# A planned attention and feed-forward kernel: DMA lags in its planner, and the first pair of heads prepared in another way

## The chip, the cores and the metric

The kernel runs on one core of a Trainium2 chip. The metric is the device time of one execution in microseconds (us).

## The reference

Attention over 4 batches with 8 heads of 64 columns and 1152 rows, with the queries averaged over pairs of rows (576 are left), then a feed-forward layer with softplus, 512 to 2048 to 512, over the 2304 rows that result:

```python
q_pool = q.reshape(B, H, S // factor, factor, D).mean(axis=3)
scores = scale * np.matmul(q_pool, k.transpose(0, 1, 3, 2))
scores = scores - np.max(scores, axis=-1, keepdims=True)
attn = np.exp(scores)
attn = attn / (np.sum(attn, axis=-1, keepdims=True) + 1e-09)
return np.matmul(attn, v).astype(np.float32)
...
h = x @ w_in
g = np.maximum(h, 0.0) + np.log1p(np.exp(-np.abs(h)))
return (g @ w_out).astype(np.float32)
```

Inputs are float64 for the weights (decoded on the chip from 64-bit words) and the weights' products are made in float16 parts, high and low, so that the result keeps float32 accuracy.

## The kernel before

**Pairs and blocks.** The work is 16 pairs of heads (u0 to u15, four to a batch) and 8 blocks of tokens. `prepare` (L629) loads keys, queries and V of a pair, finds scales from sums of squares (`scale_from_squares` L369: a matmul with ones, four small VectorE steps), and splits keys and queries into float16 parts: a high part (`hi_ways` L398, on ScalarE, GpSimd or VectorE) and a remainder (`lo_ways` L416). The parts are transposed: for pair 0 by TensorE with copies out of PSUM (`turned` L707), for the others by a DMA on the sync queue (`kT`, `qA`). The second half of the keys is copied to `kB` by two more DMAs. `kD` is the difference of two groups of four key tiles.

**Maxima and shift.** `maxima` (L797) finds an upper bound of each score row ahead of attention, nine row tiles to a pair in two halves. `row` (L808) multiplies a query tile with `kD` and with the first keys; ScalarE takes Relu of the one, and a combined VectorE pass (L822) adds the other and takes the row's maximum. `last_keys` does the ninth key tile. The negated maximum is written as two extra columns of `qlow`, which is transposed into `qB`, so that a second score matmul with `kB` takes the shift away and adds the query remainder.

**Attention.** `attention` (L928) takes a pair in two halves (256 and 320 query columns) of nine key tiles: scores on TensorE, Exp on ScalarE (L958), the product with V on TensorE (L967). Sums of the exponentials are made in one of two ways. For the pairs in `SUMMED` TensorE multiplies them with ones (L983), two steps at a time; for the others GpSimd or VectorE adds them up (`tt_ways` L431, line L435), and one matmul per half (L1038) totals the result. The sums go through three small DMAs (`few`, `scratch`, `rinv`) and come back as reciprocals. `feed_forward` splits a block, multiplies it with w_in (s<-xh,w1h and two more), takes Softplus (L1199), splits again and multiplies with w_out.

**What sets the order.** Nothing is issued by hand. Every step is a task with one or several engines it may run on, a cost for each, buffers it takes and gives, tasks it depends on and a priority. `Sched.run` (L132) plays the tasks on a model of the engines: whenever an engine is free it takes the ready task of lowest priority value, unless another engine is expected to end it sooner, and the instruction is emitted then. Its numbers are `LAG` (from the end of a task on one engine to the start of a dependent one on another), `HEAD` (how much earlier a task that uses the port shared by VectorE and GpSimd may begin before the other engine's use of it ends), `LANDS` and the cost functions. `NUDGE` shifts the priority of each kind of task of each pair or block, and `LEAN` adds to an engine's cost where a task has a choice. All engines, the sync queue among them, then run their instructions in that order and wait on semaphores. `ORDER` sets where blocks stand: u0 to u4, then block 0's first matmuls (U0), u5 and u6 with its second ones (D0), U1, and so on.

## Time and profile before

| | |
|---|---|
| Median of 3 runs | 853.09 us (852.1 to 857.29) |
| Profiled execution | 852.98 us, of which the span from first to last instruction is 851.3 us |
| Mean granted clock of TensorE | 0.989 |

In a table by stretch, the first column is the stretch in us from the span's start, then its length; then for each engine the busy time in it and the number of instructions: PE is TensorE (matmul), PEld its weight loads, DVE VectorE, ACT ScalarE, POOL GpSimd. The last three columns are the granted clock as a share of full speed, the mean busy share of the DMA engines and GB/s. A group of instructions has its line and engine, what it writes and reads, its count, and after the bar its busy time in us and the mean of one in ns. A timeline row has its start and its length in us. A line number can be that of a helper: most matmuls are issued in L363, and small VectorE steps in L352 and L355.

### The profile page before, as it was taken

Reading aid. Unit: us, or ns where it says so; the run is one execution under the profiler, and the core shown is the slowest. Engines: PE = TensorE matmul, PEld = TensorE weight load, DVE = VectorE, ACT = ScalarE, POOL = GpSimd, SP = SyncE. Lnnn points to the kernel's source line nnn. Section 1 sums busy time; section 2 is a strip of 40 time slices with the busy share of each in tenths; the row PEclk is TensorE's granted clock in tenths of the full one; section 3 lists DMA queues with packets and bytes.
Section 4 is the critical chain, followed back from the end, with each engine's and each line's share of the span. In section 5 each row is a group of like instructions: output and inputs, shape, how many; then the busy total and the mean of one; then the engine's idle time right before and its main releaser. Section 6 shows DMA issues by size and latency. Waiting matters only on the chain.

```text
span 851.3 us, 24268 instructions
## 1 busy us (share of the span) xinstructions
PE 804.3 (94%) x10250; PEld 579.0 (68%) x10250; DVE 539.0 (63%) x1171; ACT 492.8 (58%) x823; POOL 317.5 (37%) x272
## 2 busy tenths in 40 slices
PE   3898898989899999999999999999999999999997
PEld 2465566558767688768666787667876678775754
DVE  7778888889998876675685643466556626012520
ACT  4788899889897427562665545457865572120210
POOL 0105418521249201331676514611268882090000
PEclk9899999999999999999999999999999999999999
DMA  8718657358664710411652330420603000000000
GB/s 306 163 36 215 146 169 203 114 127 186 173 134 139 120 54 2 125 28 46 125 78 79 90 79 13 83 89 19 94 13 92 22 15 10 22 15 25 2 14 25
DMA packets 98093, 74.23 MB, mean 87 GB/s; under 512 B 64960, under 2 KB 79296, under 8 KB 97984
## 3 DMA queue, kind: packets, MB, share of 16 engines
q1 hardware_dynamic: 97984, 72.68, 34.6%
q8 instruction: 80, 1.31, 0.7%
q14 instruction: 29, 0.24, 0.1%
HBM read 49.81 MB, written 4.79 MB: 64 GB/s over the span
## 4 chain that ended last, share of the span: by engine, by line
PE 69%; DVE 11%; ACT 6%; DMA 5%; POOL 5%; issue 3%; SPq 1%; ACTq 0%; DVEq 0%; POOLq 0%
PE s L363 30%; PE m L363 26%; PE pv L967 12%; POOL acc L435 3%; DMA kT<-kcat 2%; ACT p L958 2%; PE pv L983 2%; DMA raw<-in_k_dram 1%; ACT raw L523 1%; DVE w L355 1%; DVE qlow L355 1%; DVE kcat L355 1%; DVE g L822 1%; PE m L1038 1%; DVE acc L435 1%
## 5 line engine op out<-in xcount | busy, mean ns | idle before, releaser
L958 ACT ACTIVATE p<-s,cols 128x512 f32<-128x512 f32 (+1 forms) x288 | 208.3, 741 | 79.1 <-PE s L363 44.0
L435 POOL TENSOR_TENSOR acc<-acc,p 128x512 f32<-128x512 f32 (+1 forms) x122 | 183.9, 1507 | 119.3 <-ACT p L958 78.1
L967 PE MATMUL pv<-p,v 128*64 128x320 f32 (+1 forms) x1152 | 189.6, 416 | 1.3 <-ACT rinv L1046 0.8
L363 PE MATMUL m<-w,gh 128*64 128x512 f16 x1152 | 175.9, 379 | 0.1
L363 PE MATMUL s<-qA,kT 128*64 128x320 f16 (+1 forms) x1152 | 159.0, 289 | 6.0 <-ACT p L958 5.5
L363 PE MATMUL s<-qB,kB 66*64 66x320 f16 (+1 forms) x1152 | 159.5, 289 | 0.0
L822 DVE CUSTOM_DVE_ANT_0 g<-m,g 128x512 f32<-128x512 f32 x144 | 98.1, 686 | 67.4 <-ACT g L818 37.4
L1199 ACT ACTIVATE g<-s,blk 128x512 f32<-128x512 f32 (+1 forms) x80 | 51.3, 642 | 148.5 <-PE s L363 113.4
L363 PEld LDWEIGHTS <-w1h 128*64 128x64 f16 x2048 | 117.6, 110 | 14.8 <-issue 1.6
L363 PE MATMUL m<-w,gl 128*64 128x512 f16 x576 | 113.5, 379 | 0.0
L363 PEld LDWEIGHTS <-gh 128*64 128x64 f16 x1152 | 71.3, 110 | 46.7 <-issue 0.7
L363 PEld LDWEIGHTS <-kT 128*64 128x64 f16 x1152 | 80.1, 111 | 31.9 <-issue 12.9
L818 ACT ACTIVATE g<-m 128x512 f32<-128x512 f32 x144 | 84.8, 596 | 26.7 <-PE m L363 22.5
L967 PEld LDWEIGHTS pv<-p,v 128*64 128x64 f32 x1152 | 77.7, 138 | 30.5 <-issue 11.2
L363 PEld LDWEIGHTS <-kB 66*64 66x64 f16 x1152 | 75.2, 111 | 19.9 <-issue 5.4
L363 PE MATMUL s<-xh,w1h 128*64 128x256 f16 (+1 forms) x1024 | 85.6, 286 | 0.3 <-ACT g L1199 0.2
L363 PE MATMUL s<-xh,w1l 128*64 128x256 f16 (+1 forms) x1024 | 85.5, 286 | 0.0
L363 PE MATMUL s<-xl,w1h 128*64 128x256 f16 (+1 forms) x1024 | 85.5, 286 | 0.0
L363 PEld LDWEIGHTS <-qA 128*64 128x64 f16 x864 | 52.6, 112 | 38.3 <-issue 20.7
L363 PE MATMUL m<-kT,qA 128*64 128x128 f16 (+1 forms) x576 | 74.7, 310 | 3.9 <-ACT g L818 2.0
L363 PE MATMUL m<-kD,qA 128*64 128x512 f16 x288 | 60.0, 397 | 5.6 <-DVE nm L822 3.4
L363 PEld LDWEIGHTS <-w1l 128*64 128x64 f16 x1024 | 59.8, 110 | 4.3
(147 smaller groups left out, 960.8 us busy)
## 6 DMA issues: line engine op xcount, KB each, us to landing
raw<-in_k_dram SPq DMA_DIRECT2D x16, 576.0 KB
v<-in_v_dram SPq DMA_DIRECT2D x16, 576.0 KB
raw<-in_q_dram SPq DMA_DIRECT2D x64, 128.0 KB
raw<-in_moe_w_out_dram SPq DMA_DIRECT2D x16, 512.0 KB
kB<-kT SPq DMA_DIRECT2D x32, 144.0 KB
gh<-in_moe_w_in_dram SPq DMA_DIRECT2D x4, 1024.0 KB
gl<-in_moe_w_in_dram SPq DMA_DIRECT2D x4, 1024.0 KB
out_dram<-g SPq DMA_DIRECT2D x16, 256.0 KB
```

What stands on the lines that cost most here:

```text
L355: nc.vector.scalar_tensor_tensor(out=out_, in0=in0, scalar=s, in1=in1, op0=op0, op1=op1)
L363: nc.tensor.matmul(out=out_[c:e], lhsT=lhsT[:, c:e], rhs=rhs, start=start, stop=stop, tile_position=(0, at + c))
L435: e.tensor_tensor(out=o, in0=a, in1=b, op=op)
L523: nc.scalar.activation(out=o, in_=i, func=ACTF.Square, accum_out=am)
L818: r = task([("ACT", act(512, 1), lambda: nc.scalar.activation(out=rest.item, in_=more.item, func=ACTF.Relu))], [y], prio, take=[rest], giv ...
L822: parts.append(task([("DVE", dve(512, 1.0, 1), lambda: nc.vector.tensor_tensor_reduce(out=rest.item, in0=most.item, in1=rest.item, scale=1 ...
L958: nc.scalar.activation(out=pt.item[:, :, 0:n], in_=s.item[:, :, 0:n], func=ACTF.Exp, scale=x.sc)
L967: nc.tensor.matmul(out=pv.item[h * 64:(h + 1) * 64, 0:n], lhsT=x.v.item[:, h, kt], rhs=pt.item[:, h, 0:n], start=(kt == 0), stop=(kt == KT ...
L983: nc.tensor.matmul(out=pv.item[g:g + 32, 512 - n // 2:512], lhsT=ones[:, 0:32], rhs=pt.item[:, h, a * n // 2:(a + 1) * n // 2], start=Fals ...
L1038: nc.tensor.matmul(out=ps.item[g:g + 32, 512 - n // 2:512], lhsT=ones[:, 0:32], rhs=acc.item[:, h, a * n // 2:(a + 1) * n // 2], start=Tru ...
L1199: x = task([("ACT", act(N, 1, 1), lambda: nc.scalar.activation(out=gs.item[:, 0:N], in_=ps.item[:, 0, 0:N], func=ACTF.Softplus, scale=ih[: ...
```

## The change

- **Lags in the planner.** The lag from an engine to a DMA falls from 1250 to 1400 ns to 60 to 150 ns, that from a DMA to an engine from 100 to 50 ns; each DMA's issue is counted 95 ns longer. `HEAD` falls from 195 (VectorE) and 330 (GpSimd) to 140; more small tasks are marked as users of the shared port. `NUDGE` and `LEAN` are replaced as a whole.
- **The first pair.** Keys and queries of pair 0 get their scales by two chains of steps instead of one.
- **Loads held.** V of later pairs, the w_in loads and the loads of pair 2 wait until the high keys of pair 0 are copied to `kB`; loads of later pairs wait until the raw buffers of the pair before are used up. The throw-away output of V's squares goes to a buffer of the exponentials (`p`) instead of a raw one.
- **Two row tiles with plain maxima.** For tiles 1 and 5 of pair 0 `whole_row` multiplies the query tile with all eight key tiles into a score buffer, and VectorE takes the maximum of 1024 columns.
- **Four summed pairs.** 0, 1, 2, 3 instead of 0, 2, 4.
- **Order of attention.** Each score task depends on the one before it and each Exp on the one before it. The scale of a block's Softplus is waited for by its first matmul instead of by the Softplus.
- **The two extra columns** of `qlow` stand ahead of the remainder instead of behind it, so a transpose reads two overlapping strips and two memsets on GpSimd go.

```diff
     LAG = {
-        "PE": {"DVE": 200.0, "ACT": 200.0, "PE": 0.0, "DMA": 1300.0},
-        "DVE": {"DVE": 40.0, "ACT": 45.0, "POOL": 60.0, "PE": 55.0, "DMA": 1400.0},
-        "ACT": {"DVE": 45.0, "ACT": 40.0, "POOL": 60.0, "PE": 55.0, "DMA": 1250.0},
-        "POOL": {"DVE": 50.0, "ACT": 60.0, "POOL": 50.0, "PE": 60.0, "DMA": 1300.0},
-        "DMA": {"DVE": 100.0, "ACT": 100.0, "POOL": 100.0, "PE": 100.0, "DMA": 150.0},
+        "PE": {"DVE": 200.0, "ACT": 200.0, "PE": 0.0, "DMA": 150.0},
+        "DVE": {"DVE": 40.0, "ACT": 45.0, "POOL": 60.0, "PE": 55.0, "DMA": 60.0},
+        "ACT": {"DVE": 45.0, "ACT": 40.0, "POOL": 60.0, "PE": 55.0, "DMA": 80.0},
+        "POOL": {"DVE": 50.0, "ACT": 60.0, "POOL": 50.0, "PE": 60.0, "DMA": 130.0},
+        "DMA": {"DVE": 50.0, "ACT": 50.0, "POOL": 50.0, "PE": 50.0, "DMA": 40.0},
     }
...
-    HEAD = {"DVE": 195.0, "POOL": 330.0}
+    HEAD = {"DVE": 140.0, "POOL": 140.0}
...
 NUDGE = {
-    "prep": [-1.5, 0, 3.75, 1, -3.25, 18.5, -0.75, 0, 0, -23.5, 26, 6.75, 0.25, 3, 6.75, 8.75],
+    "prep": [0.5, 4.25, -6.5, 0.75, 1, -15, -3, 0, 17.25, 13.25, 32.5, 0, 14.25, 35.5, 5.75, 4],
...
-    SUMMED = (0, 2, 4)
+    SUMMED = (0, 1, 2, 3)
+    PLAIN = {0:(1,5)}
...
-            390.0, 2000. * W64, last_on[g % 2], prio, [])
+            390.0, 2000. * W64, last_on[g % 2] + [units[0].kB_done], prio, [])
...
-            400.0, 2340., [], prio - 6.0, [r])
+            400.0, 2340., units[u - 1].raw_free if u > 2 else [units[0].kB_done] if u == 2 else [], prio - 6.0, [r])
...
-        both = scale_from_squares(
-            cols[:, u, 0:2], cols[:, u, 2:4], cols[:, u, 4:6], cols[:, u, 6:8], [y, z], prio)
...
+        if u == 0:
+            both = scale_from_squares(c[0], c[2], c[4], c[6], [z], prio)
+            q_scale = scale_from_squares(c[1], c[3], c[5], c[7], [y], prio)
...
-        y = task(hi_ways(1152, lambda: (qc.item, twice(qs()), c[5]), ("ACT", "DVE")), [both], prio)
+        y = task(hi_ways(1152, lambda: (qc.item, twice(qs()), c[5]), ("ACT", "DVE")), [q_scale], prio)
...
-            400.0, 2340., [], prio, [x.v])
-        jk = Hold(raw_r)
+            400.0, 2340., [units[0].kB_done] if u else [], prio, [x.v])
+        jk = Hold(p_r)
...
         def row(c, t, heads, prio):
+            if c in x.plain:
+                return whole_row(c, heads, prio)
...
+        def whole_row(c, heads, prio):
+            ps = Hold(s_r)
...
+            y = scored_by(pe(2, 512), [c], mm, [d for h in heads for e in (0, 1) for d in k_of(x, h, e)], prio, [ps], [x.qA, x.kT])
+            parts.append(task([("DVE", dve(1024), lambda: nc.vector.tensor_reduce(
+                out=x.nm3.item[:, c, 0:1], in_=ps.item.rearrange("p a b -> p (a b)"), axis=AX.X, op=ALU.max))],
+                [y], prio, give=[ps]))
...
-                e = task([("ACT", act(2 * n, 1, 1), exp, "exp")], [y, x.sc_done, *gate], prio, take=[pt], give=[s])
+                scored_last[:] = [y]
+                e = task([("ACT", act(2 * n, 1, 1), exp, "exp")], [y, x.sc_done, *gate, *in_turn], prio, take=[pt], give=[s])
                 exps.setdefault(x.u, []).append(e)
+                in_turn[:] = [e]
```

What the planner made of it, counted in the two built programs:

| Instructions | before | after |
|---|---|---|
| matmuls of exponentials with ones (TensorE) | 216 | 288 |
| additions of exponentials on GpSimd | 136 | 75 |
| additions of exponentials on VectorE | 72 | 117 |
| key differences `kD` on GpSimd / VectorE | 12 / 20 | 2 / 30 |
| all instructions on GpSimd | 277 | 194 |
| all instructions on VectorE | 1173 | 1222 |
| all instructions on ScalarE | 753 | 769 |

(A matmul in float32 stands twice in the trace, so the 216 are 432 there.)

The first place is VectorE in pair 0, from the first scale to the keys' last copy. Names: `cols` holds the scales, `raw1_73` the queries, `raw0_72` the keys, `kcat` and `qcat` the float16 parts, `kT` and `qA` the transposed keys and queries. Before:

```order
L380 RECIPROCAL cols_120<-cols_120 128x2
L352 TENSOR_SCALAR cols_120<-cols_120 128x1
L352 TENSOR_SCALAR kcat0_78<-raw0_72,cols_120 128x9x64
L352 TENSOR_SCALAR qcat0_84<-raw1_73,cols_120 128x1152
L355 SCALAR_TENSOR_TENSOR kcat0_78<-raw0_72,cols_120,kcat0_78 128x9x64 x2
L355 SCALAR_TENSOR_TENSOR qlow0_85<-raw1_73,cols_120,qcat0_84 128x9x64
L728 CAST kT0_79<-m0_108 128x512
```

After, on the same engine, from the key remainders to the scaled queries:

```order
L351 SCALAR_TENSOR_TENSOR kcat0_78<-raw0_72,cols_120,kcat0_78 128x9x64 x2
L734 CAST kT0_79<-m1_109 128x512
L348 TENSOR_SCALAR cols_120<-m2_110 128x1
L734 CAST kT0_79<-m0_108 128x512
L348 TENSOR_SCALAR cols_120<-cols_120 128x1
L432 TENSOR_TENSOR kD0_81<-kT0_79 128x512
L348 TENSOR_SCALAR cols_120<-cols_120 128x1
L734 CAST kT0_79<-m1_109 128x512
L377 RECIPROCAL cols_120<-cols_120 128x1
L432 TENSOR_TENSOR kD0_81<-kT0_79 128x512
L348 TENSOR_SCALAR cols_120<-cols_120 128x1
L348 TENSOR_SCALAR qcat0_84<-raw1_73,cols_120 128x1152
```

The scaling of the queries (`qcat`) has moved from ahead of the key remainders to behind the key copies and differences.

The second place is the sync queue from the loads of pair 1 on. `raw_74` and `raw_75` are pair 1's keys and queries, `kB_82` the high keys of pair 0. Before:

```order
L776 DMA v_76<-in_v_dram 128x2x576
L776 DMA v_77<-in_v_dram 128x2x576
L539 DMA gh<-in_moe_w_in_dram 128x4x512
L539 DMA gl<-in_moe_w_in_dram 128x4x512
L654 DMA raw_72<-in_k_dram 128x2x576
L677 DMA raw_73<-in_q_dram 128x256 x2
L681 DMA raw_73<-in_q_dram 64x128
L677 DMA raw_73<-in_q_dram 128x256 x2
L681 DMA raw_73<-in_q_dram 64x128
L743 DMA kB_82<-kT_79 64x1152 x2
```

After:

```order
L584 DMA raw_72<-in_moe_w_out_dram 128x1024
L749 DMA kB_82<-kT_79 64x1152 x2
L584 DMA raw_73<-in_moe_w_out_dram 128x1024
L538 DMA gh<-in_moe_w_in_dram 128x4x512
L538 DMA gl<-in_moe_w_in_dram 128x4x512
L783 DMA v_77<-in_v_dram 128x2x576
L770 DMA_TRANSPOSE qA_88<-qcat_84 128x9x128
L742 DMA_TRANSPOSE kT_80<-kcat_78 128x18x128
```

The weights, the second V and the loads of pair 2 have moved behind the copy of the high keys, one w_out load stands ahead of it, and pair 0's own V (not shown) ahead of pair 1's loads.

The third place is GpSimd's first additions. Before:

```order
L406 TENSOR_SCALAR kcat_78<-raw_74,cols 128x9x64
L435 TENSOR_TENSOR raw_73<-raw_73 128x9x64
L435 TENSOR_TENSOR raw_72<-raw_72 128x9x64
L435 TENSOR_TENSOR kD_81<-kT_79 128x512 x2
L406 TENSOR_SCALAR kcat_78<-raw_75,cols 128x9x64 x2
L435 TENSOR_TENSOR acc_95<-acc_95,p_93 128x2x256
L435 TENSOR_TENSOR acc_95<-acc_95,p_92 128x2x256
```

After:

```order
L403 TENSOR_SCALAR kcat_78<-raw_72,cols 128x9x64
L777 COPY qA_87<-qA_87 128x64
L403 TENSOR_SCALAR kcat_78<-raw_74,cols 128x9x64
L777 COPY qA_88<-qA_88 128x64
L432 TENSOR_TENSOR xT_66<-xT_66,rinv_97 128x256
L403 TENSOR_SCALAR kcat_78<-raw_72,cols 128x9x64
L403 TENSOR_SCALAR w1h<-raw_72,sw 128x4x256
L403 TENSOR_SCALAR kcat_78<-raw_74,cols 128x9x64
```

Pair sums, key differences and additions are gone from GpSimd's first rows; its first addition of exponentials (`acc`) now comes with pair 4.

## Rows read from the trace of the kernel before

**Rows 1.** The page's first part: span, busy time and share of each engine.

```profile
span 851.3 us, 24268 instructions
PE 804.3 (94%) x10250; PEld 579.0 (68%) x10250; DVE 539.0 (63%) x1171; ACT 492.8 (58%) x823; POOL 317.5 (37%) x272
```

**Rows 2.** Busy time of each engine by stretch.

```profile
0.00:34.00 34.00, 17.12 (x142) 9.66 (x143) 27.46 (x61) 19.26 (x34) 3.33 (x10) 0.90 0.91 262
34.00:60.00 26.00, 26.00 (x382) 17.00 (x383) 16.81 (x46) 22.03 (x36) 1.40 (x1) 1.00 0.24 70
60.00:300.00 240.00, 221.23 (x2950) 157.29 (x2948) 213.80 (x456) 196.17 (x345) 103.55 (x83) 0.98 0.62 153
300.00:440.00 140.00, 136.58 (x1792) 104.87 (x1788) 98.14 (x215) 75.94 (x120) 48.18 (x42) 1.00 0.25 62
440.00:700.00 260.00, 256.88 (x3187) 187.65 (x3185) 142.20 (x325) 156.19 (x251) 130.87 (x104) 1.00 0.28 60
700.00:852.00 152.00, 146.45 (x1814) 102.53 (x1809) 40.55 (x72) 23.22 (x39) 30.15 (x34) 0.99 0.05 16
```

**Rows 3.** TensorE's longest group of waits: total us, times, longest us.

```profile
PE m L363 <- ACT qcat L523: 11.0, 2, 8.9
```

**Rows 4.** Timeline of TensorE in pair 0: sums (L983) and products (L967).

```profile
45.52 0.65 PE L983 MATMUL pv<-p,ones 128*32 128x128 f32 x16
46.10 0.65 PE L967 MATMUL pv<-p,v 128*64 128x256 f32 x4
...
49.92 0.75 PE L983 MATMUL pv<-p,ones 128*32 128x160 f32 x16
50.60 1.30 PE L967 MATMUL pv<-p,v 128*64 128x320 f32 x8
```

**Rows 5.** Groups of instructions; the last row has ns min/median/max, first and last start.

```profile
L435 POOL TENSOR_TENSOR acc<-acc,p 128x512 f32<-128x512 f32 (+1 forms) x122 | 183.9, 1507 | 119.3 <-ACT p L958 78.1 <-ACT g L818 20.5 <-DVE acc L435 6.6
L435 DVE TENSOR_TENSOR acc<-acc,p 128x640 f32<-128x640 f32 (+1 forms) x60 | 49.5, 826 | 13.4 <-ACT p L958 8.8 <-POOL acc L435 2.8
L1038 PE MATMUL m<-acc,ones 128*32 128x128 f32 (+1 forms) x208 | 11.8, 298 | 1.0 <-DVE acc L435 1.0
L435 DVE TENSOR_TENSOR kD<-kT 128x512 f16<-128x512 f16 x20 | 12.2, 633 | 1.3 <-DMA kT<-kcat 1.3
...
L355 DVE SCALAR_TENSOR_TENSOR kcat<-raw,cols,kcat x32: 778/811/2103, 12.3 to 647.7; 128x576 f16<-128x576 f32 x32
```

**Rows 6.** Timeline of the start, pair 0, to the first scores.

```profile
4.85 1.16 ACT L523 ACTIVATE kcat<-raw 128x1152 f16<-128x1152 f32 x1 [2.77 <-DMA raw<-in_k_dram]
...
7.32 0.76 DVE L435 TENSOR_TENSOR raw<-raw 128x576 f32<-128x576 f32 x1 [1.36 <-DMA raw<-in_q_dram]
...
8.94 0.38 PE L363 MATMUL m<-cols,ones 128*64 128x2 f32 x4 [8.94 <-ACT qcat L523]
...
10.17 0.77 ACT L402 ACTIVATE kcat<-raw,cols 128x576 f16<-128x576 f32 x1 [1.28 <-DVE cols L380]
...
10.96 1.40 DVE L352 TENSOR_SCALAR qcat<-raw,cols 128x1152 f16<-128x1152 f32 x1
...
14.46 0.88 DVE L728 CAST kT<-m 128x512 f16<-128x512 f32 x2
...
17.04 0.64 PE L363 MATMUL m<-kD,qA 128*64 128x512 f16 x2 [0.21 <-DVE kT L728]
...
25.28 0.68 DVE L822 CUSTOM_DVE_ANT_0 g<-m,g 128x512 f32<-128x512 f32 x1
...
25.89 0.69 DVE L838 TENSOR_REDUCE nm<-m 128x4 f32<-128x512 f32 x1
...
32.09 0.47 PE L363 MATMUL s<-qA,kT 128*64 128x256 f16 x2
```

**Rows 7.** Timeline of the sync queue (SPq): two DMAs of a chain of sums.

```profile
52.78 0.33 SPq L1058 DMA_DIRECT2D scratch<-few  x1
54.19 0.55 SPq L1061 DMA_DIRECT2D rinv<-scratch  x1
```

More of the change, by code (lines that the diff above doesn't have):

```diff
@@ L53 @@
-        "split": [-100, -2200, 0, -1950, 1150, 0, 250, -200],
-        "up": [1050, 400, -150, 0, 850, -100, -2300, 100],
-        "down": [0, 0, 100, -1350, 50, 1800, -50, 650],
+        "prep": [-500, -50, 100, -50, -50, 2050, 1750, -350, 450, 0, 100, -450, 450, -0, -1000, 150],
+        "value": [3400, 350, 1250, -1600, 2950, -100, 450, 350, -800, -5850, -1950, -650, 0, 0, 0, 400],
+        "most": [-200, -2200, 100, 0, -4100, 250, -1350, 50, -1000, 100, -100, 2700, 0, 650, 1400, -650],
+        "shift": [-100, 1800, -1650, 300, -0, 200, 1300, 0, 1850, 0, 750, -400, -300, 100, 0, -700],
@@ new lines @@
+        "close": [2200, -1500, 700, -2250, 50, 150, -300, 1700, -100, 0, -1200, -100, 0, 100, 0, 1000],
+        "win": [-750, 0, 3800, 950, -850, -2500, 150, -2450],
+        "wout": [-600, 0, 0, -250, 2050, 1850, 300, 3950, -300, 0, 0, -150, 1850, 1500, 0, 2600],
+        "wparts": [250, -850, 1450, -650, -350, -550, 1200, 0, -400, 2400, 750, 1050, 400, -450, 300, -800],
+        "split": [-100, -650, 1350, 450, -650, 950, 0, 4950],
+        "up": [3550, 950, -2350, -150, -1850, -1450, -2400, -150],
@@ L72 @@
+        "down": [2400, 50, -1350, -250, 4600, 0, -150, -3600],
     },
@@ L222, in run @@
                         else:
-                            wire = max(max(now + 390.0, wire) + tag, done + 75.0)
+                            wire = max(max(now + 390.0, wire) + tag, done - 20.0)
                         done = wire + self.LANDS
@@ L250, in pool1 @@
 def pool1(n):
-    return 145.0 + n * 0.95
+    return 250.0 + n * 0.86
 def pool2(n):
@@ L364, in tiled, with small @@
                              tile_position=(0, at + c))
-    def small(fn, deps, prio, n=1, take=(), give=()):
-        return task([("DVE", 165.0 + 20.0 * (n > 1), fn)], deps, prio, take=take, give=give)
+    def small(fn, deps, prio, n=1, take=(), give=(), port=False):
+        way = ("DVE", 165.0 + 20.0 * (n > 1), fn)
+        return task([way + ("port",) if port else way], deps, prio, take=take, give=give)
     def scale_from_squares(am, t, s, inv, deps, prio):
@@ L439, in load @@
     def load(fn, queue, wire, deps, prio, take):
-        return task([("DMA", queue, fn, wire)], deps, prio, take=take)
+        return task([("DMA", queue + 95.0, fn, wire)], deps, prio, take=take)
     ORDER = ("u0", "u1", "u2", "u3",
@@ L523, in on_act @@
             nc.scalar.activation(out=o, in_=i, func=ACTF.Square, accum_out=am)
-        return task([("ACT", act(n), on_act)], [dep], prio, take=take, give=give)
+        return task([("ACT", 105.0 + (act(n) if n in (576, 1152) else 212.0 + n * 0.924), on_act)], [dep], prio,
+                    take=take, give=give)
     def staged(n):
@@ L706, in prepare @@
         r.users = 2
+        x.raw_free = list(parts)
         def turned(src, dst, tiles, deps, prio, give):
@@ L735, in prepare @@
         else:
-            x.k_done = [task([("DMA", 2000.0, lambda: nc.sync.dma_start_transpose(
+            x.k_done = [task([("DMA", 2095.0, lambda: nc.sync.dma_start_transpose(
                 out=x.kT.item, in_=cat.item.rearrange("p t d -> p (t d)")), 1150.0, 1700.0)], parts, prio,
@@ L868, in maxima, with low_rows @@
         x.qB_done = [[], []]
+        def low_rows(out_, c, rhs, start, stop):
+            for lo in (0, STRIP):
+                nc.tensor.matmul(out=out_[lo:lo + STRIP], lhsT=x.low()[:, c, 2 - lo // 32:D + 2 - lo // 32], rhs=rhs,
+                                 start=start, stop=stop, tile_position=(0, lo))
         for half, h in ((0, None), (1, 0), (1, 1)):
@@ L1227, in tile_attention_softplus_ffn @@
             nc.vector.memset(kb[D:D + 2], SHIFT)
-        if ROWS > D + 2:
-            for low in qlow_r.free:
-                nc.gpsimd.memset(low[:, T * (D + 2):], 0.0)
         sd.run()
```

166 lines of the change are left out of this document (82 added, 84 removed).

## The prediction

> **What bounds the kernel now.** I read the page's busy times first, then a table by stretch, then TensorE's waits, then the start and single rows. The profiled execution took 852.98 us (span 851.3 us, 1.7 us around it); the three runs have a median of 853.09 us, so the two stand for each other. TensorE is busy for 804.3 us of the span, 94%; the next engine, VectorE, for 63% [rows 1]. So the sum has two parts: what TensorE gets more or less to do, and what of its 47 us of idle time goes or comes. The reader is to see in the table by stretch where these 47 us lie [rows 2]: 16.9 us before 34 us (34 less 17.12); nothing from 34 to 60; 18.8 us from 60 to 300 (240 less 221.23); 3.4 us from 300 to 440; 3.1 us from 440 to 700; 5.5 us in the last stretch, where the last output tile is drained and stored, which the change does not touch. In the stretch from 60 to 300, VectorE is busy for 213.8 and ScalarE for 196.2 of 240 us: that is where pairs are still prepared and weights are decoded beside attention, and TensorE waits there in many short pieces. Of all its waits only the first is long: 11.0 us behind ScalarE's squares, 8.9 of them at the start; no other group of waits has more than half of that, and none ends on a DMA [rows 3].
>
> **The change part by part.**
>
> *A fourth summed pair.* Pairs 0, 1, 2, 3 instead of 0, 2, 4 have their sums of exponentials made by TensorE. For two steps of 256 columns the sixteen small matmuls take 0.58 us (45.52 to 46.10), for two steps of 320 columns 0.68 us (49.92 to 50.60) [rows 4]. A pair has nine steps of each: 9 x 0.29 + 9 x 0.34 = 5.7 us. The two totals of a pair that is not summed go: 11.8 us for 13 pairs, 0.9 us [rows 5]. TensorE gets **+4.8 us** (4 to 6). In return 16 additions go, 1.5 us each on GpSimd or 0.83 us on VectorE [rows 5], and they go where both are needed, in pairs 1 and 3, while pair 4 has to do its own again.
>
> *The first pair.* Before, the scales of keys and queries were made together, so the keys (squared from 4.85 us on) waited for the queries' pair sums at 7.32 us; the first scaled keys stand at 10.17 us [rows 6]. Apart, the keys' square ends at 6.1 us, and with the same 1.23 us from the scale's matmul to the first scaling (8.94 to 10.17) the keys can be scaled at 7.4 us, 2.7 us earlier. But the queries do not gain that. By the order VectorE now does three copies of transposed keys (two of them take 0.88 us in a row), two key differences and the queries' small steps before it scales the queries (1.40 us). I put that at 3.2 us behind the key remainders, which end at about 9.8 us, so the scaled queries are there at 14.4 us (an estimate from these rows) instead of 12.36 us; their transposes, which opened TensorE's work before, now close it. The first maxima matmul then starts at about 15.6 us instead of 17.04 us, since the keys' 36 transposes lie behind it already. So of 2.7 us about 1.4 us are left.
>
> *Two row tiles with plain maxima.* TensorE does as many columns as before. ScalarE loses two Relu passes; VectorE's combined pass (0.68 us) becomes a maximum over 1024 columns. No row shows that; a maximum over 512 takes 0.69 us [rows 6], so the price lies between 0.69 and 1.38 us, and I take 1.2 us, near the upper end, as the columns double: +1.0 us on VectorE for both. It is paid by the scaling of pair 1, which stood in the middle of these maxima (1.40 us and a key remainder) and now is ScalarE's or later. By the order the remaining matmuls between the first half's shift and the first scores shrink from three row products and ten small ones to one and two. So the first scores come at about 28.5 us instead of 32.09 us. The second half's shift has as much VectorE work ahead of it as before, which is what limits this: I take **-3.0 us** at the start (-1.2, the gain at the first maxima, to -5).
>
> *Loads held.* Weight loads, V of later pairs and the loads of pair 2 wait until the high keys of pair 0 are copied. On the sync queue everything behind that copy waits with it: weights and V of pair 1. These stood before it and now leave some 3 us later; their readers, ScalarE's decode and V's squares, stand behind most of the first maxima in ScalarE's order, so I cost it at nothing; without that cover the decode would be up to 3 us late. One w_out load stands ahead of the copy and waits for the first raw buffer, free when the key remainders are done, before the copy can start anyway.
>
> *True DMA lags and new tables.* The lags are numbers in the planner. What they do is a new order for every engine: by the count of instructions 61 additions leave GpSimd (136 to 75), 45 of them to VectorE (72 to 117; the fourth summed pair takes the other 16), and ten of the twelve key differences that GpSimd did go to VectorE too. The old plan added 1.25 to 1.4 us between an engine and a DMA that follows it. The trace shows how long such a step is: a reciprocal frees the write of the few sums at 52.78 us, and the next DMA, which reads them back, starts at 54.19 us, 1.41 us from issue to issue with 0.33 us of issue in it [rows 7]; the plan's landing of 1.34 us was already that, so the added lag was counted twice. A plan that knows this can put work closer behind its data. It acts where the queue and VectorE are both busy, from 60 to 300 us. There 18.8 us of idle TensorE are to be had at most. The nearest row to a lower bound is VectorE's own: it is idle for 26.2 us there [rows 2], and by the order 11 more additions and 8 more key differences stand on it before block 1's last split, about 11 x 0.83 + 8 x 0.63 = 14.2 us [rows 5]. For it speaks that GpSimd's share falls: a key remainder takes 0.81 us at the median but up to 2.10 us [rows 5], and I take it that the long ones lie beside GpSimd's work. I take **-7 us**, a bit over a third of the idle time (-14 to +8). For 400 to 700 us, where 6.5 us are idle and VectorE is little over half busy, I take **-1 us** (-4 to +3).
>
> The Trainium skill (DMA: Bandwidth & Descriptors, Anatomy of one DMA) gives a DMA a fixed cost of about 2.0 us, most of it the receipt of the last byte; it says so of the path that GpSimd issues, and this kernel issues on the sync queue. By that price each DMA of a chain would land 0.6 us later than the 1.41 us of this trace, and the new plan would be too tight; the row disagrees where the queue is idle, and the last rival below has the case in which it is not.
>
> **The sum:** 852.98 + 4.8 - 3.0 - 7.0 - 1.0 = **846.8 us**, 0.7% less. The likeliest case alone reaches from 842 to 850 us.
>
> **The rivals.**
> 1. *The plan fits.* The start gives 5 us and the stretch to 300 us loses most of its idle time (14 us), the later one 3 us: 852.98 + 4.8 - 5 - 14 - 3 = 835.8 us. For it: TensorE's waits there are short pieces that a better order can fill. Against it: ScalarE and VectorE are both over 80% busy there, and there is 5 us more for TensorE to place. 0.20.
> 2. *Nothing comes of it.* The start gives its 3 us, the plan 2 us, the fourth summed pair takes 4.8 us: 852.8 us. For it: the second half of pair 0 is no earlier, and the idle time hangs on VectorE and ScalarE, not on DMAs; no wait of TensorE ends on a DMA. 0.25.
> 3. *VectorE becomes the bound (slower).* Of the 14.2 us that it gets more before block 1's last split, half finds no idle time, and pairs 5 and 6 get their shifts late: 852.98 + 7.1 + 4.8 - 3 = 861.9 us. It decides from the point where VectorE can use less than half of its 26.2 idle us; at 89% busy now that is near. Against it: the additions are low in priority and fill gaps. 0.09.
> 4. *The lags are too short where the queue is loaded.* DMAs in a full queue land later than alone; the five early pairs that are transposed by DMA then make TensorE wait for the dropped 1.25 us each, and the plan gives nothing: 852.98 + 4.8 - 3 - 1 + 6.3 = 860.1 us. For it: DMA engines are 62% busy in that stretch [rows 2]. Against it: transposes stand well ahead of use. 0.06.
>
> **How the numbers follow.** The forecast has 0.40. The range, 835 to 859 us, holds rivals 1 and 2 and leaves out the slower ends. A change of under 1% (844.5 to 861.6 us) is about what a measurement of this kernel can't tell from none. Faster by over 1%: rival 1 and the lower third of the forecast, 0.20 + 0.15 = 0.35. Slower by over 1%: most of rival 3 and a little of rival 4, 0.07. Within 1%: 0.58.
>
> **What would show it.** First scores near 28.5 us in the timeline (right) or after 31 us (the start gives nothing). TensorE's idle time from 60 to 300 us: near 12 us by the forecast, under 6 by rival 1, over 20 with VectorE at 95% by rival 3, and waits of TensorE or its weight loads that end on a DMA by rival 4. The matmuls with ones should go from 432 to 576 and cost about 5.7 us. GpSimd's busy time should fall by about 90 us. The prediction is wrong if the idle time of TensorE after 300 us moves by more than 4 us, since nothing there was counted on.

## The result, and the profile after

The changed kernel takes **825.0 us** (median of four runs, 823.36 to 825.46) against 854.32 us of the kernel before, measured beside it: a ratio of **0.9651, 95% interval 0.9616 to 0.9687**. The prediction had 846.8 us and a range of 835 to 859. The direction was right, the size was not: from the one profiled execution to the other (852.98 to 825.36 us) 28 us came of it where 6 were forecast.

The page's first part, of the kernel after; it answers to [rows 1]:

```profile
span 823.2 us, 24500 instructions
PE 798.4 (97%) x10382; PEld 567.4 (69%) x10382; DVE 527.5 (64%) x1220; ACT 505.7 (61%) x839; POOL 195.3 (24%) x189
```

The span is 28.1 us shorter. TensorE's idle time fell from 47.0 to 24.8 us (span less busy time), its busy time by 5.9 us although it does more matmuls. The table by stretch, of the kernel after, shows where; it answers to [rows 2]:

```profile
0.00:34.00 34.00, 19.45 (x208) 12.50 (x212) 28.16 (x63) 22.12 (x37) 3.23 (x10) 0.95 0.80 240
34.00:60.00 26.00, 26.00 (x383) 16.61 (x384) 21.66 (x50) 24.30 (x42) 0.73 (x1) 1.00 0.44 136
60.00:300.00 240.00, 235.65 (x3300) 169.96 (x3298) 209.27 (x511) 183.84 (x322) 58.23 (x54) 1.00 0.58 141
300.00:440.00 140.00, 138.85 (x1788) 101.92 (x1786) 97.15 (x211) 97.27 (x160) 41.88 (x34) 1.00 0.35 85
440.00:700.00 260.00, 260.00 (x3338) 189.08 (x3336) 144.91 (x342) 152.75 (x242) 86.84 (x82) 1.00 0.22 56
```

From 60 to 300 us, 4.35 us of TensorE's time are idle instead of 18.8, and in that stretch it does 3300 matmuls instead of 2950. (The stretches are equal in time and not in work: the kernel after is further on at 300 us.) Before 34 us it lost 2.3 us of idle time, from 300 to 440 another 2.3, from 440 to 700 all of 3.1. GpSimd is busy for 195 instead of 318 us. TensorE's waits, of the kernel after (engine, tile and line, what it waited for; total us, times, longest), answer to [rows 3]:

```profile
PE m L359 <- ACT kcat L521: 6.1, 1, 6.1
PE m L359 <- DVE qcat L348: 2.7, 1, 2.7
PE m L359 <- POOL kcat L403: 2.3, 1, 2.3
PE m L359 <- ACT g L828: 2.0, 3, 1.1
```

The three longest are single waits of the start. The start itself, as a timeline of the kernel after (start, length); it answers to [rows 6]:

```profile
4.75 1.16 ACT L521 ACTIVATE kcat<-raw 128x1152 f16<-128x1152 f32 x1 [2.67 <-DMA raw<-in_k_dram]
...
6.06 0.38 PE L359 MATMUL m<-cols,ones 128*64 128x1 f32 x4 [6.06 <-ACT kcat L521]
...
7.25 0.78 ACT L399 ACTIVATE kcat<-raw,cols 128x576 f16<-128x576 f32 x1 [1.25 <-DVE cols L377]
...
13.72 1.40 DVE L348 TENSOR_SCALAR qcat<-raw,cols 128x1152 f16<-128x1152 f32 x1
...
16.51 0.64 PE L359 MATMUL m<-kD,qA 128*64 128x512 f16 x2 [0.16 <-ACT qA L731]
...
27.25 0.30 PE L359 MATMUL s<-qA,kT 128*64 128x256 f16 x2
```

Keys are scaled at 7.25 us and the first scores start at 27.25 instead of 32.09. The groups of the kernel after that answer to [rows 5], and the sums of the four pairs (mean ns behind the busy time):

```profile
L432 POOL TENSOR_TENSOR acc<-acc,p 128x512 f32<-128x512 f32 (+1 forms) x67 | 97.2, 1450 | 139.5 <-ACT p L987 89.2
...
L432 DVE TENSOR_TENSOR acc<-acc,p 128x640 f32<-128x640 f32 (+1 forms) x101 | 76.8, 760 | 13.2 <-ACT p L987 10.5
...
L1014 PE MATMUL pv<-p,ones 128*32 128x128 f32 (+1 forms) x576 | 25.9, 293 | 0.0
L1069 PE MATMUL m<-acc,ones 128*32 128x128 f32 (+1 forms) x192 | 10.9, 298 | 0.0
```

One place is not in any row ahead of the prediction, and the experiments lead to it: when the raw buffers are loaded. The sync queue's loads of a pair's keys, of the kernel before, the fourth to the eighth:

```profile
28.35 0.54 SPq L654 DMA_DIRECT2D raw<-in_k_dram  x1
69.41 0.59 SPq L654 DMA_DIRECT2D raw<-in_k_dram  x1
121.64 0.38 SPq L654 DMA_DIRECT2D raw<-in_k_dram  x1
191.04 0.38 SPq L654 DMA_DIRECT2D raw<-in_k_dram  x1
213.31 0.43 SPq L654 DMA_DIRECT2D raw<-in_k_dram  x1
```

The same five loads in the kernel after:

```profile
69.17 0.58 SPq L654 DMA_DIRECT2D raw<-in_k_dram  x1
96.81 0.54 SPq L654 DMA_DIRECT2D raw<-in_k_dram  x1
126.60 0.59 SPq L654 DMA_DIRECT2D raw<-in_k_dram  x1
158.72 0.54 SPq L654 DMA_DIRECT2D raw<-in_k_dram  x1
190.44 0.39 SPq L654 DMA_DIRECT2D raw<-in_k_dram  x1
```

Before, the fourth pair's keys came at 28 us and then the gaps were 41, 52, 69 and 22 us. After, each of these follows the one before by 28 to 32 us. The weights of w_out are loaded into the same buffers, in sixteen parts (count, ns min/median/max, first and last start). Before:

```profile
L585 SPq DMA_DIRECT2D raw<-in_moe_w_out_dram x16: 323/332/535, 78.5 to 233.4; - x16
```

After, they begin 68 us earlier:

```profile
L584 SPq DMA_DIRECT2D raw<-in_moe_w_out_dram x16: 323/332/897, 10.4 to 208.6; - x16
```

### The profile page after: what moved, and what is told of

The parts are those of the page before. It is cut to its first block, busy times and chain, and to the rows that moved or that the text cites. A ratio compares the mean times of both kernels' runs of the same rounds, so it can differ in the third digit from the quotient of the medians.

```text
span 823.2 us, 24500 instructions
## 1 busy us (share of the span) xinstructions
PE 798.4 (97%) x10382; PEld 567.4 (69%) x10382; DVE 527.5 (64%) x1220; ACT 505.7 (61%) x839; POOL 195.3 (24%) x189
## 4 chain that ended last, share of the span: by engine, by line
PE 88%; DVE 5%; ACT 2%; issue 2%; DMA 1%; POOL 1%; SPq 0%; DVEq 0%; ACTq 0%; POOLq 0%
PE s L359 38%; PE m L359 30%; PE pv L998 15%; PE pv L1014 3%; DMA raw<-in_k_dram 1%; DVE acc L432 1%; PE m L1069 1%; DVE g L832 1%; PE m L898 1%; DVE kcat L351 1%; ACT kcat L521 1%; ACT p L987 1%; DVE qlow L351 1%; ACT g L828 0%; POOL acc L432 0%
## 5 line engine op out<-in xcount | busy, mean ns | idle before, releaser
L987 ACT ACTIVATE p<-s,cols 128x512 f32<-128x512 f32 (+1 forms) x288 | 210.7, 742 | 71.1 <-PE s L359 40.2
L359 PE MATMUL m<-w,gh 128*64 128x512 f16 x1152 | 173.5, 379 | 0.0
L1230 ACT ACTIVATE g<-s,blk 128x512 f32<-128x512 f32 (+1 forms) x80 | 51.5, 645 | 140.1 <-PE s L359 131.7
L432 POOL TENSOR_TENSOR acc<-acc,p 128x512 f32<-128x512 f32 (+1 forms) x67 | 97.2, 1450 | 139.5 <-ACT p L987 89.2
L359 PEld LDWEIGHTS <-w1h 128*64 128x64 f16 x2048 | 113.5, 110 | 19.9 <-issue 2.0
L359 PEld LDWEIGHTS <-gh 128*64 128x64 f16 x1152 | 66.9, 110 | 52.1 <-issue 1.6
L359 PEld LDWEIGHTS <-kT 128*64 128x64 f16 x1152 | 77.8, 111 | 29.2 <-issue 9.6
L359 PEld LDWEIGHTS <-kB 66*64 66x64 f16 x1152 | 72.4, 110 | 19.1 <-issue 4.3
L432 DVE TENSOR_TENSOR acc<-acc,p 128x640 f32<-128x640 f32 (+1 forms) x101 | 76.8, 760 | 13.2 <-ACT p L987 10.5
L351 DVE SCALAR_TENSOR_TENSOR gl<-g,blk,gh 128x512 f16<-128x512 f32 (+1 forms) x72 | 50.1, 700 | 44.5 <-ACT gh L399 40.4
L359 PE MATMUL m<-kT,qA 128*64 128x512 f16 (+1 forms) x572 | 70.2, 302 | 1.4 <-ACT g L828 0.7
```

The source lines that it names most:

```text
L351: nc.vector.scalar_tensor_tensor(out=out_, in0=in0, scalar=s, in1=in1, op0=op0, op1=op1)
L359: nc.tensor.matmul(out=out_[c:e], lhsT=lhsT[:, c:e], rhs=rhs, start=start, stop=stop, tile_position=(0, at + c))
L432: e.tensor_tensor(out=o, in0=a, in1=b, op=op)
L987: nc.scalar.activation(out=pt.item[:, :, 0:n], in_=s.item[:, :, 0:n], func=ACTF.Exp, scale=x.sc)
L1230: x = task([("ACT", act(N, 1, 1), lambda: nc.scalar.activation(out=gs.item[:, 0:N], in_=ps.item[:, 0, 0:N], func=ACTF.Softplus, scale=ih[: ...
```

## The experiments

**Two theories.** S: the code (what waits for what, which buffers are used, the planner's lags and prices) carries the gain. T: the new tables, `NUDGE` and `LEAN`, carry it. To tell them apart, most kernels have all of `NUDGE` and `LEAN` set to zero ("flat"), since tables fitted to one plan are no fair test of another. In the diffs below `EDGE` stands for `units[u - 1].raw_free if u > 2 else []`, the dependency that holds a pair's key and query loads until the pair before has used up its raw buffers; the kernel after has it, and the text calls it the edge. Beside these runs the kernel before had medians from 853.3 to 854.9 us, so 1 to 2 us between rows of the table mean little.

| run | kernel | median us | ratio to before, 95% interval |
|---|---|---|---|
| e1 | before, flat | 914.1 | 1.0685 (1.0636 to 1.0735) |
| e2 | after, flat | 841.9 | 0.9856 (0.9823 to 0.9889) |
| e3 | before, flat, new lags | 876.6 | 1.0261 (1.0229 to 1.0292) |
| e4 | after, flat, old lags | 835.7 | 0.9787 (0.975 to 0.9824) |
| e5 | after, flat, three summed pairs | 847.9 | 0.992 (0.9897 to 0.9942) |
| e6 | after, flat, V's squares in the raw ring | 859.4 | 1.0074 (1.0051 to 1.0096) |
| e7 | after, flat, no holds behind pair 0 | 848.2 | 0.9924 (0.9898 to 0.9949) |
| e8 | after, flat, old prices | 838.7 | 0.9827 (0.9738 to 0.9917) |
| e9 | before, flat, V's squares out of the ring | 877.6 | 1.025 (1.0211 to 1.0289) |
| e10 | after with tables, V's squares in the ring | 871.3 | 1.0189 (1.0165 to 1.0213) |
| e11 | after, flat, without the edge | 867.9 | 1.0145 (1.0119 to 1.0171) |
| e12 | after with tables, old lags and prices | 854.5 | 0.9993 (0.9969 to 1.0017) |
| e13 | before, flat, squares out, edge | 856.2 | 1.0023 (1.0002 to 1.0043) |
| e14 | before, flat, edge | 862.6 | 1.0079 (1.0049 to 1.0109) |
| e15 | as e13, new lags | 860.3 | 1.0071 (1.0045 to 1.0096) |
| e16 | as e15, four summed pairs | 857.1 | 1.0032 (1.0009 to 1.0054) |
| e17 | before with its tables, squares out, edge | 863.3 | 1.0109 (1.0073 to 1.0144) |
| e18 | after, flat, start of before | 840.1 | 0.9836 (0.9811 to 0.9861) |

**Code or numbers: e1 to e4.** The edit of e1 and e2, at each of the two codes:

```diff
 NUDGE = {
-    "prep": [-1.5, 0, 3.75, 1, ...
+    "prep": [0, 0, 0, 0, ...
```

> The kernel before with both tables (priority shifts and engine leanings) set to zero. All theories: slower than 853 us, since nothing is tuned. It is the base line for the next three. I expect 880 to 910 us.

> The changed kernel with both tables set to zero. Theory S (the code parts carry the gain: four summed pairs, first pair apart, loads held, raw buffers, true lags): at least 20 us faster than the kernel before with zero tables. Theory T (the newly searched tables carry it): within 8 us of it, and the 28 us come only with the tables.

e3 puts the new `LAG`, landing times and issue costs into e1, e4 the old ones into e2. `HEAD`, which the two expectations name among them ("port heads", "heads"), stayed in both as it was, so no run tells what it gives.

> The kernel before with zero tables and only the new DMA lags, port heads and issue costs in the planner. Theory L (the lags are what matters): 10 us or more faster than the kernel before with zero tables. Theories S and T: within 6 us of it, since no wait of TensorE ended on a DMA.

> The changed kernel with zero tables and the old lags, heads and issue costs. Theory L: 10 us or more slower than the changed kernel with zero tables, near the kernel before with zero tables. Theory S in its other parts: within 6 us of the changed kernel with zero tables.

Without tables the two codes are 72 us apart (914.1, 4 us above what was expected, and 841.9), so theory S holds: the new code without any table is already 12 us faster than the old one with its own. Each set of tables then takes off what it can, 60 us from the old and 17 us from the new. The lags are worth 37 us to the old code, and in the new one the old lags are 6 us *faster*. So beside the rest of the new code they give nothing.

**Which part of the code: e5 to e8.** Each undoes one part of e2. e5, three summed pairs:

```diff
-    SUMMED = (0, 1, 2, 3)
+    SUMMED = (0, 2, 4)
```

> The changed kernel with zero tables, and three summed pairs (0, 2, 4) as before. Theory Q (the fourth summed pair, which empties GpSimd's and VectorE's additions out of the first 200 us, is the part that pays): 12 us or more slower than the 842 us of the changed kernel with zero tables. Theory R (the raw buffers and what holds the loads): within 5 us of it, 4.8 us of matmuls less included.

e6, the throw-away output of V's squares back in a raw buffer (the view of it changes with it):

```diff
-        jk = Hold(p_r)
+        jk = Hold(raw_r)
```

> The changed kernel with zero tables, and the throw-away output of V's squares in a raw buffer again instead of a buffer of the exponentials. Theory R: the ring of four raw buffers is short, so loads and weight decoding come late, 12 us or more slower than 842 us. Theory Q: within 5 us.

e7, no load waits for the high keys of pair 0 (one of the four places):

```diff
-            390.0, 2000. * W64, last_on[g % 2] + [units[0].kB_done], prio, [])
+            390.0, 2000. * W64, last_on[g % 2], prio, [])
```

> The changed kernel with zero tables, and no load waits for the copy of pair 0's high keys. Theory R: the start is 2 to 6 us slower, the rest the same. Theory Q: within 3 us.

e8, the old prices of GpSimd and ScalarE and the old marks of the shared port (the list of the change names the marks but not the prices, which it changes too; one of the places):

```diff
-    return 250.0 + n * 0.86
+    return 145.0 + n * 0.95
```

> The changed kernel with zero tables, and the planner's old prices of GpSimd's and ScalarE's work and its old marks of who uses the shared port (the new lags stay). Theory C (the prices keep work off GpSimd and this pays): 12 us or more slower than 842 us and GpSimd busy for over 140 us. Theories Q and R: within 5 us.

The fourth summed pair is worth 6.0 us and the holds 6.4 (1.0 and 0.4 us beyond what theory R allowed them; theory Q asked for 12 and more of the one), the new prices nothing (the old ones are 3 us faster, within the interval). The largest is the throw-away output of V's squares: back in one of the four raw buffers it costs 17.5 us. The squares themselves cost the same in either place (mean 1159 ns to a raw buffer before, 1161 ns to a `p` buffer after); what costs is the buffer that they hold.

**The raw ring: e9 to e12.** The four raw buffers, a ring from which each task takes a free one, serve keys, queries, the decoding of w_in, the weights of w_out and, before, V's squares. e9 takes the squares out of the flat kernel before; e10 is the reverse, in the kernel after with its tables:

```diff
-        jk = Hold(raw_r)
+        jk = Hold(p_r)
```

> The kernel before with zero tables and its own long lags (914 us), with one line changed: V's squares write their throw-away output into a buffer of the attention's p ring, as the kernel after does, and no longer into one of the four raw buffers. Theory R (the raw ring is the part of the code that counts: in the kernel after, giving it back to the squares cost 17.5 us): the time falls by 15 us or more, to 900 us or less, and TensorE in 60 to 300 us is busy for over 182 us instead of 174.7. Theory J (the parts help only together: fewer key sums on VectorE, held loads and the freed ring): within 5 us of 914.

> The kernel after with all its tables, and only V's squares' throw-away output back in a raw buffer. Theory R (the freed raw ring is a limit that no order gets round): slower by 12 us or more, 837 us or more. Rival (a table can order the squares round the ring; the flat plan only could not): within 5 us of 825. A table made for another plan can also be worse by itself, so a result over 850 us would not be read as the ring's price.

e11 takes the edge out of e2, here for the keys, and in the same way for the queries:

```diff
-            400.0, 2340., units[u - 1].raw_free if u > 2 else [units[0].kB_done] if u == 2 else [], prio - 6.0, [r])
+            400.0, 2340., [units[0].kB_done] if u == 2 else [], prio - 6.0, [r])
```

> The kernel after with zero tables (842 us) and without the edge that holds a pair's loads of keys and queries until the pair before it has given its raw buffers back. Theory R (what matters is that loads do not stand on the sync queue waiting for a raw buffer, and the edge keeps them off it): slower by 5 us or more. Rival (with V's squares gone from the ring the edge has nothing left to do): within 3 us of 842.

e12 has the edits of e4 and of e8 in the kernel after with its tables.

> The kernel after with its tables, but with the long lags, the old queue costs and the old prices and port marks of the planner; each of these was faster by 3 to 6 us with zero tables. Theory T (the tables were fitted to the plan that the new numbers make): slower than 825 us by 5 us or more, near the 836 us of the flat plan with old lags or above it. Rival (the old numbers are simply better): 815 to 823 us, faster than both kernels.

The one line of e9 takes 36.5 us off the old code. How, is not shown: its first w_out load is no earlier than in e1 (130.6 and 113.7 us), and its key loads stay uneven. e11's rival said that with the squares gone the edge has nothing left to do; it fell, the edge is worth 26.0 us there. Why shows in the third to the sixth key load of e11, and between them the copy of pair 0's high keys:

```profile
10.30 0.38 SPq L654 DMA_DIRECT2D raw<-in_k_dram  x1
11.42 2.12 SPq L749 DMA_DIRECT2D kB<-kT  x2
...
30.18 0.53 SPq L654 DMA_DIRECT2D raw<-in_k_dram  x1
...
80.89 0.40 SPq L654 DMA_DIRECT2D raw<-in_k_dram  x1
...
103.08 0.43 SPq L654 DMA_DIRECT2D raw<-in_k_dram  x1
```

At 10 us, where e2 loads the first part of w_out, e11 loads the keys of one more pair. They can't be u2's, which by e11's code still wait for the copy that is issued at 11.42 us; so they are those of u3 or a later pair, which overtakes u2 and takes its room in the ring. e11 thus prices the edge beside the hold of u2, and not by itself. What then gets no buffer is w_out. Its loads in e11:

```profile
L584 SPq DMA_DIRECT2D raw<-in_moe_w_out_dram x16: 322/336/578, 136.0 to 242.0; - x16
```

And in e2, which differs by the edge alone:

```profile
L584 SPq DMA_DIRECT2D raw<-in_moe_w_out_dram x16: 322/328/744, 10.2 to 197.7; - x16
```

With the edge, w_out is read from 10 us on in the gaps between pairs; without it not before 136 us, and then all sixteen come within 106 us. e10 and e12 were slower by 46 and 29.5 us, far more than the same edits cost flat (e6 17.5; e4 and e8 faster by 6 and 3). Tables fit one plan, and under another they can be worse than none (e10 against e6: 871.3 and 859.4 us): neither says what its edit costs. That the old numbers might simply be better (e12's rival) is refuted for these tables.

**Do the two explain the difference of the codes: e13 to e16.** The edge goes into the flat kernel before, with and without the freed ring.

```diff
-            400.0, 2340., [], prio - 6.0, [r])
+            400.0, 2340., EDGE, prio - 6.0, [r])
...
-        ql = load(load_q, 3100.0, 2600., [], prio - 6.0, [qr])
+        ql = load(load_q, 3100.0, 2600., EDGE, prio - 6.0, [qr])
...
+        x.raw_free = list(parts)
...
+        x.raw_free.append(x.ql_done)
```

> The kernel before with zero tables and its long lags (914 us), with two things of the new code: V's squares out of the raw ring (877.6 us alone) and the edge that holds the key and query loads of pair 3 and later until the pair before has given its raw buffers back. Theory R (the raw ring is the whole matter): 840 to 853 us, within 11 us of the flat new code's 842, and the first loads of w_out before 60 us instead of after 113. Theory J (the edge helps only beside the holds, the split start and the fourth summed pair): over 865 us.

> As e13, but with the edge alone; V's squares stay in the raw ring. Theory R: the edge keeps pair loads from filling the ring whatever else sits in it, so most of the gain comes: 855 to 875 us (the new code with the squares in the ring and with the edge has 859.4). Rival (both are needed): within 10 us of 914.

> As e13, with the short lags and new queue costs. In the old code they gave 37 us, in the new one they cost 6. Theory R (in the old code they helped only because shorter lags free raw buffers earlier in the plan): within 8 us of e13. Rival (the lags are worth something by themselves): faster than e13 by 15 us or more.

> As e15, with four summed pairs (0 to 3) in place of three. In the new code the fourth was worth 6 us net. If the same holds here: 3 to 9 us faster than e15; if it was worth something only in that one plan: within 3 us, or slower by up to the 4.8 us that it adds to TensorE.

The edge alone takes the old code from 914.1 to 862.6 us; V's squares out of the ring add 6.4, to 856.2 (alone, in e9, they gave 36.5). Together that is 58 of the 72 us between the codes. e13 is 3 us over its window, so the ring is most of the matter and not the whole; its first w_out load is at 27 us. The stretch from 60 to 300 us in three parts, in e1 (columns as in the table by stretch):

```profile
60.00:140.00 80.00, 73.40 (x968) 49.49 (x966) 53.34 (x121) 61.39 (x106) 25.83 (x22) 1.00 0.56 112
140.00:220.00 80.00, 53.37 (x652) 33.41 (x650) 74.00 (x157) 59.78 (x108) 24.59 (x21) 0.85 0.65 177
220.00:300.00 80.00, 47.96 (x582) 36.76 (x582) 59.38 (x130) 28.88 (x52) 3.02 (x4) 0.76 0.28 88
```

The same in e14:

```profile
60.00:140.00 80.00, 70.66 (x918) 46.38 (x914) 65.41 (x141) 66.84 (x122) 24.93 (x19) 0.98 0.63 156
140.00:220.00 80.00, 70.61 (x938) 49.87 (x937) 70.69 (x152) 59.58 (x104) 33.83 (x28) 0.94 0.56 139
220.00:300.00 80.00, 70.99 (x834) 51.15 (x835) 66.66 (x128) 54.81 (x97) 34.86 (x27) 0.96 0.40 89
```

In e1 VectorE is busy for only 53 of the first 80 us and for 74 of the next, and TensorE idles for 27 and 32 us in the second and third part; its sixth key load is at 79.6 us, its seventh at 179.8. With the edge the work of both is level. With both edits in, the new lags change nothing for the better (860.3 against 856.2), where alone they gave 37 us: the three overlap. That the lags too work through the ring is not shown: in e3 the sixth and seventh key load are as far apart (82.6 and 185.3 us) and the first w_out load is at 135.5 us. The fourth summed pair gives 3.2 us here, at the lower end of what was expected.

**The old tables, and the start: e17 and e18.**

e17 has the edits of e13 in the kernel before with its own tables.

> The kernel before with its own tables and lags (854 us), V's squares out of the raw ring, and the edge. Theory R: the ring was a limit that its tables could not get round, so the time falls below 846 us. Rival (tables fitted to another plan are worse than none): slower than the flat plan with the same two edits, 856 us.

e18, in the flat kernel after:

```diff
-    PLAIN = {0:(1,5)}
+    PLAIN = {}
...
-        if u == 0:
+        if u < 0:
```

The second line puts the two scales of pair 0 back into one.

> The kernel after with zero tables (842 us), with the start of before: scales of pair 0's keys and queries made together, and no row tile with plain maxima; the holds stay. The prediction's term: 3 us slower (1.2 to 5), first scores 3 us later. Rival (what the start loses is made up in the busy stretch after it): within 1 us.

e17 took 863.3 us, as its rival said: with the two edits the old tables are worse than no tables (856.2), and worse than the old tables without the edits. So the gain of the freed ring does not come on top of tables that were fitted without it. What the old code gives with the two edits and tables made anew was not tried. e18 took 840.1 us against e2's 841.9, with intervals that overlap. Its first scores start at 30.09 us against 27.76 in e2, so the new start does bring attention forward by 2.3 us; the end does not notice. TensorE is idle for 1.9 us less before 34 us in e2 and for 2.4 us more from 60 to 300: what the start gains is lost in the busy stretch behind it.

No kernel tried here beats the 825.0 us of the change.

## Why the prediction was wrong

**The step that failed** is in *Loads held*. It priced the waits for pair 0's high keys, "I cost it at nothing", and left the rest of that edit without a price: the wait of later pairs' loads for the raw buffers of the pair before, and V's squares leaving the raw ring. Without tables those two make 58 of the 72 us between the codes; undone one at a time in the new code they cost 26.0 (beside the hold of u2) and 17.5. For the two kernels with their tables this is argued and not shown, since undoing a part there also spoils the fit of the tables (e10); what their traces show is that key loads became even and that the loads of w_out begin 68 us earlier. A wait that is added to a load reads like a cost. Here it is the gain: it keeps a load that is not needed yet out of a buffer that another needs now. Rows that point there were to be had: the uneven key loads shown above, and in the chain of waits of the kernel before the longest piece that is not TensorE's, a key load that took 12.6 us to land, issued right behind three loads of w_out (211.1 to 213.3 us):

```profile
213.31 12.64 DMA raw<-in_k_dram
```

The Trainium skill (Perfetto Trace Analysis, Optimization Strategy) says that bubbles that repeat on the engine that should be saturated can mean that there is too little SBUF for the next tile to be allocated. The runs show a near case: no buffer was added, and by the edge alone, which changes who gets the four, TensorE's idle time from 60 to 300 us went from 65.3 us (e1) to 27.7 (e14).

**By terms.** The sum came out 21.9 us too high (846.8 against 824.9 us, the span after and the 1.7 us around it). The stretch from 60 to 300 us has 7.4 of them, the time after 300 us 4.4, the clock, for which the sum had no term, up to 6.9, and at least 4.0 are left over; the start gave 0.7 us less than taken and the summed pair cost 0.2 more.

**The plan from 60 to 300 us, -7 us.** The place was right, and so was the bound (18.8 us of idle time, of which 14.4 went; the term's own lower end was -14). The reason given, that "the added lag was counted twice", holds for the old code alone, where the new lags gave 37 us (e3). Beside the other edits it fails: in e4 the old lags were 6 us faster, in e15 the new ones 4 us slower. The two DMAs of [rows 7] were also a short case: 1.08 us of their 1.41 were waiting. The sync queue's waits for that step, of the kernel before (total us, times, longest):

```profile
SPq L1061 <- DMA scratch<-few: 32.5, 20, 4.6
```

And of the kernel after:

```profile
SPq L1092 <- DMA scratch<-few: 45.6, 22, 5.1
```

The mean wait is 1.6 us before and 2.1 after, so with the 0.33 us of issue some 2.0 and 2.4, an estimate from these rows. The Trainium skill (DMA: Bandwidth & Descriptors, Anatomy of one DMA) gives a DMA of the path that GpSimd issues a fixed cost of about 2.0 us; both means lie nearer to it than the 1.41 us that the prediction took. None of TensorE's longer waits after ends on a DMA, so rival 4 fell as it was put; whether lags that are too short are what made the new ones 4 to 6 us slower in e4 and e15, no run tells.

**The start, -3 us.** The keys were scaled when forecast (7.25 against 7.4 us), the queries at 15.1 (13.72 and 1.40) instead of 14.4, the first maxima at 16.5 instead of 15.6, the first scores at 27.25, earlier than the 28.5 forecast; the maximum over 1024 columns took 1.22 us, as taken. As TensorE's idle time it gave 2.3 us. By e18 it is worth nothing to the end. Here the silent step failed that time won ahead of a stretch with waits is won at the end.

**The fourth summed pair, +4.8 us.** As TensorE's work this was right: the sums went from 20.0 us to 25.9, the totals from 11.8 to 10.9, +5.0 us together. As a term it had the wrong sign. Flat, it makes the kernel 6.0 us faster (e5) and 3.2 in the old code (e16). The likely reason, which no run takes apart, is that what it takes off GpSimd and VectorE in the busy stretch is worth more than it costs; the sum had no number for that.

**Later, -1 us.** From 300 to 700 us, 5.4 us of idle time went, beyond the term's -4 and beyond the 4 us that the prediction named as its own mark for being wrong. (The mark's reason, that nothing was counted on there, does not go with a term of -1 us.)

**What the sum left out.** TensorE's busy time fell by 5.9 us instead of rising by 5. One reason is its clock, for which [rows 2] had a granted clock of 0.90 and 0.98 in the first and third stretch and the sum had nothing. Stretches of the kernel before (the third column from the right is the granted clock):

```profile
26.00:34.00 8.00, 7.12 (x52) 3.73 (x52) 7.42 (x21) 6.41 (x12) 0.63 (x1) 0.57 0.91 206
64.00:70.00 6.00, 3.57 (x62) 2.40 (x58) 4.34 (x10) 5.11 (x10) 1.68 (x2) 1.00 1.20 216
70.00:75.00 5.00, 4.82 (x36) 2.96 (x38) 4.43 (x13) 4.08 (x9) 4.40 (x4) 0.66 1.04 314
98.00:105.00 7.00, 4.20 (x64) 2.35 (x59) 5.16 (x12) 5.81 (x11) 2.53 (x2) 1.00 0.93 245
105.00:109.00 4.00, 3.71 (x38) 2.56 (x37) 3.13 (x6) 4.00 (x7) 0.00 (x0) 0.57 0.14 54
180.00:184.00 4.00, 4.00 (x31) 1.81 (x30) 2.98 (x7) 1.81 (x3) 1.48 (x1) 0.57 0.26 64
```

And the only such stretch of the kernel after:

```profile
27.00:32.00 5.00, 4.80 (x62) 4.09 (x61) 4.68 (x12) 3.58 (x6) 0.24 (x1) 0.66 1.01 179
```

After TensorE had been idle for 2.4 of 6 us and for 2.8 of 7, a stretch followed with a granted clock of 0.66 and 0.57, mostly the lower of its two levels (1.2 and 2.4 GHz). Length times what is missing from 1.00 makes 8.6 us in the four stretches before and 1.7 in the one after: up to 6.9 us. So these idle gaps cost more than their length. The remaining 4.0 us or more (-5.9, less 5.0, plus 6.9) no run here takes apart. With 852.98 + 5.0 - 22.2 - 6.9 - 4.0 = 824.9 us the sum closes, but only because the 4.0 are what was left.

**The rivals.** Rival 1 (the plan fits, 835.8 us, under 6 us idle) was the right one by its mark, 4.35 us idle, at a chance of 0.20 against 0.40 for the forecast; its 22 us of idle time are the 22.2 that went, with less at the start and more later. It was 11 us too slow by the clock and those 4 us. Rival 2 fell. Rival 3 fell at its point: VectorE has more additions (101 for 60) and yet was idle for 30.7 us in that stretch instead of 26.2.

**What stays open.** Of the 72 us between the flat codes 14 are not the ring's. Holds (6.4) and the fourth summed pair (3 to 6) make some of that, and lags, prices and start, by the runs, took 4 to 11 off it again; so some 6 to 16 us belong to parts that were not tried alone, such as the order of scores and Exps, `HEAD` and the two extra columns, if the parts add up, which the edge and the squares do not (51.5 and 36.5 alone, 58 together). And no run tells how much of the last 17 us, 841.9 to 825.0, each entry of the new tables gives.

## What to carry over

When several kinds of loads share a ring of buffers and one queue, list the times of each kind's loads before trusting any engine's busy time: even gaps at the pace of the consumer are healthy, an early bunch followed by a long gap can mean that one kind has taken the ring. A wait added to a load that comes too early can be worth more than any faster step, and an output that is thrown away should not sit in the scarcest ring. Judge such an edit with the fitted tables set to zero on both sides, and refit after it: tables made for the old ring took 60 us off it, and under the new one they cost 7 us.

## What the hardware showed that was not expected

VectorE got 45 more additions (41 of them onto a running sum, as in the rows) and ten of GpSimd's twelve key differences, and its busy time fell by 11.5 us. A good part of that is work that left it: high parts of the Softplus over 512 columns (`gh`), 21 before and 7 after, and products with the reciprocals (`xT`), 20 and 11. But its two-input steps also got shorter where GpSimd did less: an addition over 640 columns took 932 ns before and 821 after, a key remainder 1036 and 906. The Trainium skill (SBUF — State Buffer, Who interferes with whom) says that a VectorE instruction with two inputs in SBUF contends with GpSimd instructions that read SBUF; the trace agrees for these. The additions over 512 columns took 687 and 690 ns; that they too can pay shows in e17, where GpSimd is busy for 314 us and they took 769 ns, those over 640 columns 981. Of GpSimd's busy time 122 us went, 90 were forecast. The forms, of the kernel after:

```profile
L432 DVE TENSOR_TENSOR acc<-acc,p 128x640 f32<-128x640 f32 x54 | 44.3, 821 | 7.5 <-ACT p L987 6.7
L432 DVE TENSOR_TENSOR acc<-acc,p 128x512 f32<-128x512 f32 x47 | 32.4, 690 | 5.7 <-ACT p L987 3.8 <-POOL acc L432 1.2
L351 DVE SCALAR_TENSOR_TENSOR kcat<-raw,cols,kcat 128x576 f16<-128x576 f32 x32 | 28.0, 906 | 1.2 <-POOL kcat L403 0.9 <-ACT kcat L399 0.3
...
L847 DVE TENSOR_REDUCE nm<-s 128x1 f32<-128x1024 f32 x2 | 2.4, 1217 | 0.0
```
